# Attention feeding two feed-forward layers on one core: transfers of one tile ordered together, a 64-query product that waits to be seen, running sums stored later, last output tiles in other buffers

## The chip, the cores and the metric

One Trainium2 chip, one of its NeuronCores. The time of a run is device microseconds of that core for one execution of the whole program; the median of several runs is given. The trace is that of one profiled execution.

A core has engines that run their own instruction streams side by side: TensorE (PE in the profile; its weight loads are PEld), VectorE (DVE), ScalarE (ACT), GpSimd (POOL) and SyncE (SP). SP computes nothing here; it issues transfers between HBM and on-chip memory, one after the other, on its own queue (SPq). A few transfers are issued by ACT (ACTq). Each stream is in order: an instruction that waits holds all that stand behind it on its engine. Matmuls write to eight PSUM banks.

## The reference

```python
# q, k, v: (4, 8, 576, 64); s: (4, 8, 576)
cum    = np.cumsum(np.maximum(s, 0.0), axis=-1)
bias   = -(cum[:, :, :, None] - cum[:, :, None, :])
scores = np.where(causal, -1e9, scale * q @ k.T + np.minimum(bias, 0.0))
attn   = softmax(scores);  x = attn @ v          # laid out as (2304 tokens, 512)
x = (x @ w_a * (x @ w_b)) @ w_out                # d_ff 1536
h = x @ w_in                                     # d_ff 2048
out = (np.maximum(h, 0) + alpha * np.minimum(h, 0)) @ w_out2
```

## The kernel before

**Blocks and steps.** The 2304 tokens go through the feed-forward layers in four blocks (512, 512, 512 and 768 tokens). Of every batch of 576 queries, the first 512 belong to a block of their own; the last 64 of all four batches belong to the last block. The first batch's attention runs alone at the start. After it, the attention of later batches is cut into some dozens of steps a block that are put between the feed-forward matmuls of the block before: scores (`s01`, `s23` for 512 queries, `s4` for the last 64, L744), the product with the values (`av`, L804; `av_b` for the 64 queries, L862), all per batch and pair of heads. Every feed-forward matmul is done as three (high by high, low by high, high by low: L1223 to L1225, L1854 to L1856, L1706 to L1708). The last block uses seven products of half-size blocks in place of eight for part of its work.

**The path of a 64-query tile.** `s4` gives scores in PSUM; DVE and ACT make probabilities `z`; DVE turns them in 32x32 blocks into `zt`; SP stores `zt` to a scratch `zd` in HBM and loads it back in another layout as `pb`; `av_b` multiplies `pb` with the values in `vb`. The tile `vb` for a 64-query product is filled by six transfers: four of 32x4x128 (64 KB), two of 32x128 (16 KB). Also loaded on SP: `kq` (queries and keys of a pair of heads), `cb` (running sums, broadcast; `cb0` and `cb1` for the 512 and for the 64 queries), `pt` (as `pb`, for the 512 queries), and `raw` (weights).

**What sets the order.** Nothing schedules at run time. While the program is written out, the class `Order` keeps a clock for each engine from a table of costs and plays the steps through. Work off PE is written as generators (chains): each `yield` names an engine and a cost, and the planner emits the instruction when that engine is next free in its plan. `dma` (L315) takes 480 ns of SP and counts as landed after a planned latency; a chain that fills a tile by several `yield from dma(...)` lines emits the next transfer only after the one before has landed in the plan, and transfers of other chains are emitted between them. `due` (L1259) emits the attention steps that are due among the feed-forward matmuls; it puts a step off by up to four steps while `possible` (L1234) says that the plan has not seen its inputs yet. Before the change `possible` answers yes for `av_b` alone at once: `av_b` is emitted when it is due, and the planned clock is moved on to the time at which its inputs are there. In the program that runs, order is all that is left of the plan: each engine runs its list, with waits on semaphores.

**Eight lanes.** A transfer's landing is signalled on one of eight semaphores (`DMAHW0` to `DMAHW7` in the order's waits) in turn; a transfer on SP waits, before it is issued, until the one before it on its lane has landed.

**Start and end.** `first_attention` stores the running sums `cum` to `cum_d` in HBM (L387) right after DVE has made them, between the loads of `kq`. At the end six output tiles are copied from PSUM to tiles `o` of one tag (`t`, four slots) by ACT and stored by SP; the fifth and the sixth wait until the stores of the first two have landed.

Of the kernel before, what the change touches and what calls it, by code (L numbers as in the profile page):

```python
# [21 lines left out]
P = 128  # L22
D = 64
# [188 lines left out]
def attention_two_moe_kernel(  # L212
# [102 lines left out]
    def dma(o, i):  # L315
        yield {"sp": 480}, 700
        nc.sync.dma_start(o, i)
        yield {"dma": prod(o.shape) / (180 if o.dtype == U16 else 90)}, run.landing

    def split(src, hi, lo, sbuf=True):  # L320
        yield from copy(hi, src, 0.52 if sbuf else 1.04)
        yield from sub(lo, src, f32(hi), sbuf)
# [61 lines left out]
    def running_sums(s_sb):  # L384
        nc.vector.tensor_scalar(s_sb, s_sb, 0.0, 8.0, op0=ALU.max, op1=ALU.mult)
        nc.vector.tensor_tensor_scan(cum[:, 0:S], s_sb, s_sb, 0.0, op0=ALU.add, op1=ALU.max)
        nc.sync.dma_start(cum_d, cum[:, 0:S])  # L387
        nc.vector.tensor_copy(cum[:, S:S + QB], cum[:, QA:S])
        for i in range(0, P, D):
            nc.scalar.activation(cums[i:i + NE], cum[0:NE, 0:QA], AF.Copy)  # L390
            if i == 0:
                nc.vector.tensor_tensor(
                    cums[BH:BH + NE], cum[0:NE, 0:QA], f32(cums[0:NE]), op=ALU.subtract
                )
            else:
                nc.vector.tensor_copy(cums[i + BH:i + BH + NE], f32(cums[BH:BH + NE]))
        bases = acc[3][:, 0:4 * NE].rearrange("p (r b) -> p r b", b=NE)
        for r in range(4):
            nc.tensor.matmul(
                bases[:, r, :], cum[:, r * P:r * P + 1].to_broadcast([BH, P]), ident[:BH, 0:NE],  # L400
                start=True, stop=True,
            )
        nc.vector.scalar_tensor_tensor(
            rows, bases, less[:, 0:1], one_of, op0=ALU.mult, op1=ALU.add
        )
        sums = acc[2][:, 0:NR * BH].rearrange("p (r b) -> p r b", b=BH)
        for r in range(NR):
            nc.tensor.transpose(sums[:, r, :], cum[:, r * P:(r + 1) * P], ident[:BH, :BH])
        nc.vector.tensor_scalar(cumq[:, 0:4, :], sums[:, 0:4, :], -1.0, None, op0=ALU.mult)
        for j in range(2):  # L410
            own = slice(j * QB, (j + 1) * QB)
            nc.vector.tensor_scalar(
                cumq[own, 4, 0:BH // 2], sums[own, 4, j:BH:2], -1.0, None, op0=ALU.mult
            )
# [2 lines left out]
    sizes = [512] * (NT // 512 - 1) + [512 + NT % 512]  # L417
    NB = len(sizes)

    def leave(b, t, o):  # L420
        if t < QA // P:
            yield from dma(out[b * S + t * P:b * S + (t + 1) * P, :], o)
        else:
            ends = [(2 * t - 2 * QA // P + j + 1) * S for j in range(2)]
            halves = [
                run.spawn(dma(out[e - QB:e, :], o[j * QB:(j + 1) * QB]), run.t)
                for j, e in enumerate(ends)
            ]
            for half in halves:
                yield half  # L430
        run.give(of_t, run.t)


    pb_t, scores = {}, []
# [16 lines left out]
    def load_v(b, hp, u):  # L451
        c0 = 2 * hp * D
        got = []

        def chain():
            yield of_vb
            vr = raw.tile([P, 5, 2 * D], F32, name="vb", tag="vb", bufs=VB)
            got.append(vr)
            if b + u >= TURN:
                keys = v[b, 0:QA, c0:c0 + 2 * D].rearrange("(c j k) d -> j k c d", j=4, k=32)  # L460
                if u:
                    yield {"pool": 240}, SEEN
                    nc.gpsimd.memset(vr[:, 4, :], 0.0)
                for j in range(4):
                    yield from dma(vr[j::4, 0:4, :], keys[j])
                    if u and j < 2:
                        k0 = QA + 32 * j
                        yield from dma(vr[j::4, 4, :], v[b, k0:k0 + 32, c0:c0 + 2 * D])
                return
            yield from dma(  # L470
                vr[:, 0:4, :], v[b, 0:QA, c0:c0 + 2 * D].rearrange("(c p) d -> p c d", p=P)
            )
            if u:
                yield {"pool": 240}, SEEN
                nc.gpsimd.memset(vr[QB:P, 4, :], 0.0)
                yield from dma(vr[0:QB, 4, :], v[b, QA:S, c0:c0 + 2 * D])

        v_t[b, hp, u] = got, run.spawn(chain(), slack=SL_QK)

# [19 lines left out]
    def load_kq(b, hp, u):  # L499

        got = []

        def chain():
            if not u and b >= STACK:
                halves = [run.spawn(stack(b, 2 * hp + j, got), run.t) for j in range(2)]
                yield halves[0]
                yield halves[1]
                return
            yield of_kq
            kq = raw.tile([P, 2 * QA], F32, name="kq", tag="kq", bufs=KQ)  # L510
            got.append(kq)
            if u:
                yield from dma(kq[:, 0:S + P], kq_b[b, hp])
            else:
                for j in range(2):
                    own = slice(j * D, (j + 1) * D)
                    yield from dma(kq[own], kq_a[b, 2 * hp + j, own])

        kq_t[b, hp, u] = got, run.spawn(chain())

    def load_sums(b, h, u):

        got = []

        def chain():
            yield of_c1 if u else of_c0
            nk = S if u else QA
            cb = raw.tile([P, nk], F32, name=f"cb{u}", tag=f"cb{u}", bufs=2 if u else CB)
            got.append(cb)
            n = P // (u + 1)  # L530
            for j in range(u + 1):
                bh = b * H + (u + 1) * h + j
                yield from dma(
                    cb[j * n:(j + 1) * n], cum_d[bh:bh + 1, 0:nk].to_broadcast([n, nk])
                )

        cb_t[b, h, u] = got, run.spawn(chain())

# [278 lines left out]
        parts = (x[b % 2][:, hp, :] for x in (xh, xl))  # L817
        x_done[b].append(read_by(at, split(pv, *parts, False)))

    def t4(b, hp, j):  # L820

        if j == 0:
            z_t[b, hp, 4] = probabilities(b, hp, 4)
        z = z_t[b, hp, 4]
        k, n = (QB, P) if j else (P, QA)
        at = slot()
        tp = banks[at][0:k, 0:n]
        for c in range(n // P):
            k0 = j * QA + c * P
            nc.tensor.transpose(tp[:, c * P:(c + 1) * P], z[:, k0:k0 + k], ident)  # L830
        run.pe(n / P * 107)
        if j:
            z_t.pop((b, hp, 4))
            run.give(of_z[4])

        def chain():
            if j == 0:
                yield of_pb
                pb_t[hp] = raw.tile([P, 5 * P], F32, name="pb", tag="pb")
                yield {"pool": 240}, SEEN  # L840
                nc.gpsimd.memset(pb_t[hp][QB:P, QA:5 * P], 0.0)
            o = j * QA
            yield from copy(pb_t[hp][0:k, o:o + n], tp, 1.04)

        e_t[b, hp, 4 + j] = read_by(at, chain())

    def av_b(b, hp):

        turned = b + 1 >= TURN
        if turned:  # L850
            settle((b, hp, 4))
        else:
            run.need(*(e_t.pop((b, hp, 4 + j)) for j in range(2)))
        got, ready = v_t.pop((b, hp, 1))
        run.need(ready)
        pb = pb_t.pop(hp)
        at = slot()
        pv = banks[at][:, 0:QB]
        for c in range(5 if turned else 0):
            for j in range(2):  # L860
                p = pb.rearrange("p (i t n) -> p i t n", i=4, n=32)
                nc.tensor.matmul(  # L862
                    pv[64 * j:64 * j + 64], got[0][:, c, j * D:(j + 1) * D],
                    p[:, 2 * j:2 * j + 2, c, :], start=c == 0, stop=c == 4,
                )
        for c in range(0 if turned else 5):
            for j in range(2):
                o = c * P + j * QB
                nc.tensor.matmul(
                    pv[64 * j:64 * j + 64], got[0][:, c, j * D:(j + 1) * D], pb[:, o:o + QB],  # L870
                    start=c == 0, stop=c == 4,
                )
        run.pe(5 * 107)
        run.give(of_vb)
# [11 lines left out]
    def first_attention():  # L886
# [12 lines left out]
        for i in range(HP + 2):  # L899
# [14 lines left out]
                s23(0, i, 3)  # L914
            if i == FROM_WEIGHTS:
                nc.sync.dma_start(alpha_sb, alpha)
                ahead = AHEAD
                prefetch()
            if i == FROM_LEAD:
# [312 lines left out]
        return all(c.done and c.time <= run.now + 100 for c in chains)  # L1232

    def possible(f, args):  # L1234
        rings = 1 if f == two_av else 2
        if f not in (s01, s23, s4, two_av):
            return True
        if not seen(*(reader[i] for i in ring[:rings] if i in reader)):
            return False
        if f == two_av:  # L1240
# [3 lines left out]
                v_t[a, hp, 0][1], v_t[b, hp, 1][1]  # L1244
            )
        b, hp = args[:2]
        if f == s4:
            return seen(kq_t[b, hp, 1][1], z_t[b, hp, 4][1])
        r = args[2] if f == s23 else 0
# [169 lines left out]
    def ffn_seven(blk, sums):  # L1419
# [226 lines left out]
            return end  # L1646

        def store(t):
            yield of_t
            o = ft.tile([P, DM], F32, name="o", tag="t")  # L1650
            yield from copy(o, (acc + banks[0:2])[t], 1.04, SHRUNK ** 2)
            run.spawn(leave(blk, t, o), run.t)

        def x2_part(o, j, d, c):
            yield from split_by(o, xh[1 - j][:, d, c], xl[1 - j][:, d, c], SHRUNK ** 2)
# [98 lines left out]
    def ffn(blk):  # L1754
# [57 lines left out]
        def store(t):  # L1812
            yield of_t
            o = ft.tile([P, DM], F32, name="o", tag="t")
            yield from copy(o, acc[t], 1.04, SHRUNK ** 2)
            run.spawn(leave(blk, t, o), run.t)

        for f in range(NF1 + 1):
            if f < NF1:
# [140 lines left out]
```

## Time and profile before

| | before |
|---|---|
| median of 3 runs | 991.97 us (991.25 to 992.36) |
| profiled execution | 991.26 us, its span 989.5 us |
| PE busy | 964.1 us, 97% of the span |
| DVE / ACT / POOL busy | 745.3 / 559.3 / 231.9 us |
| mean granted TensorE clock | 0.992 of full speed |
| chain that ended last | PE 94%, DVE 2%, DMA 2%, ACT 2% |

The span runs from the first to the last instruction; the run is 1.8 us longer. Read the share of the chain first, then the list of what PE waited for, then the stretches around these waits. The granted clock is given as a share of full speed: 1.00 is 2.4 GHz, 0.50 is 1.2 GHz. A row of the timeline is: start, busy time, engine, line, operation, output<-input and count, and in brackets the idle time before it and what ended it.

### The profile page before, as it was taken

Reading aid. Unit: us, or ns where it says so; the run is one execution under the profiler, and the core shown is the slowest. Engines: PE = TensorE matmul, PEld = TensorE weight load, DVE = VectorE, ACT = ScalarE, POOL = GpSimd, SP = SyncE. Lnnn points to the kernel's source line nnn. Section 1 sums busy time; section 2 is a strip of 40 time slices with the busy share of each in tenths; the row PEclk is TensorE's granted clock in tenths of the full one; section 3 lists DMA queues with packets and bytes.
Section 4 is the critical chain, followed back from the end, with each engine's and each line's share of the span. In section 5 each row is a group of like instructions: output and inputs, shape, how many; then the busy total and the mean of one; then the engine's idle time right before and its main releaser. Section 6 shows DMA issues by size and latency. Waiting matters only on the chain.

```text
span 989.5 us, 15862 instructions
## 1 busy us (share of the span) xinstructions
PE 964.1 (97%) x5235; PEld 811.8 (82%) x5235; DVE 745.3 (75%) x1725; ACT 559.3 (57%) x1162; POOL 231.9 (23%) x291
## 2 busy tenths in 40 slices
PE   6999999999999999969999999999999999999997
PEld 5577777788888888858888888888899999999896
DVE  7897878868788878847578868666497888788772
ACT  6976767657665657526455547544552333566443
POOL 2130113321155556303235434522100000000000
PEclk9999999999999999979999999999999999999999
DMA  7589997789599978977498786855403223021202
GB/s 191 179 283 320 344 364 248 280 291 320 202 285 297 319 247 280 283 222 231 151 273 252 214 273 195 252 177 176 161 24 105 65 64 103 27 65 65 64 0 65
DMA packets 140115, 196.78 MB, mean 199 GB/s; under 512 B 35776, under 2 KB 79808, under 8 KB 140032
## 3 DMA queue, kind: packets, MB, share of 16 engines
q1 hardware_dynamic: 130240, 177.93, 57.5%
q10 hardware_dynamic: 9792, 17.83, 4.9%
q8 instruction: 41, 0.67, 0.3%
q14 instruction: 42, 0.34, 0.1%
HBM read 152.13 MB, written 43.59 MB: 198 GB/s over the span
## 4 chain that ended last, share of the span: by engine, by line
PE 94%; DVE 2%; DMA 2%; ACT 2%; issue 0%; SPq 0%; ACTq 0%
PE bank L1223 21%; PE bank L1224 21%; PE bank L1225 21%; PE bank L1854 5%; PE bank L1856 4%; PE bank L1855 4%; PE bank L804 3%; PE bank L1707 2%; PE bank L1706 2%; PE bank L1708 2%; PE bank L547 2%; PE bank L744 1%; PE bank L566 1%; PE bank L862 1%; DMA kq<-in_kq_a_dram 1%; ACT z L276 1%
## 5 line engine op out<-in xcount | busy, mean ns | idle before, releaser
L1223 PE MATMUL bank<-xh,wh 128*128 128x512 f32 (+1 forms) x620 | 237.8, 384 | 0.0
L1224 PE MATMUL bank<-xl,wh 128*128 128x512 f32 (+1 forms) x620 | 234.3, 378 | 0.9 <-DVE xl L292 0.9
L1225 PE MATMUL bank<-xh,wl 128*128 128x512 f32 (+1 forms) x620 | 234.1, 378 | 0.0
L284 ACT ACTIVATE wh<-raw 128x512 fp32r<-128x512 f32 (+1 forms) x198 | 115.0, 592 | 91.8 <-PE bank L1224 39.0
L1223 PEld LDWEIGHTS bank<-xh,wh 128*128 128x128 f32 x620 | 116.5, 188 | 25.7 <-issue 6.5
L1224 PEld LDWEIGHTS bank<-xl,wh 128*128 128x128 f32 x620 | 116.6, 188 | 19.9 <-DVE xl L292 1.4
L1225 PEld LDWEIGHTS bank<-xh,wl 128*128 128x128 f32 x620 | 116.5, 188 | 19.4
L301 POOL TENSOR_TENSOR wl<-raw,wh 128x512 fp32r<-128x512 f32 x68 | 92.1, 1359 | 114.7 <-ACT wh L284 82.8
L301 DVE TENSOR_TENSOR wl<-raw,wh 128x512 fp32r<-128x512 f32 (+1 forms) x136 | 84.4, 633 | 39.9 <-ACT wh L284 33.6
L276 ACT ACTIVATE z<-z,mn 128x512 f32<-128x512 f32 (+4 forms) x144 | 83.0, 578 | 36.9 <-DVE mn L292 36.2
L1223 PE MATMUL bank<-gh,wh 128*128 128x512 f32 (+1 forms) x240 | 89.6, 373 | 0.0
L1224 PE MATMUL bank<-gl,wh 128*128 128x512 f32 (+1 forms) x240 | 88.6, 369 | 0.0
L1225 PE MATMUL bank<-gh,wl 128*128 128x512 f32 (+1 forms) x240 | 88.4, 368 | 0.0
L1854 PE MATMUL bank<-wh,gh 128*128 128x512 f32 x192 | 77.8, 405 | 0.0
L284 ACT ACTIVATE gh<-g 128x512 fp32r<-128x512 f32 x84 | 52.8, 628 | 43.1 <-DVE g L292 42.8
L1856 PE MATMUL bank<-wh,gl 128*128 128x512 f32 x192 | 75.5, 393 | 0.0
L1855 PE MATMUL bank<-wl,gh 128*128 128x512 f32 x192 | 75.5, 393 | 0.0
L1004 ACT ACTIVATE top<-raw 128x512 f16<-128x512 bf16 x90 | 69.2, 785 | 7.1 <-DMA raw<-in_w_dram 3.8
L301 DVE TENSOR_TENSOR gl<-g,gh 128x512 fp32r<-128x512 f32 x68 | 51.6, 759 | 18.4 <-ACT gh L284 17.5
L301 POOL TENSOR_TENSOR wl<-w,wh 128x512 fp32r<-128x512 f32 x24 | 31.8, 1323 | 134.8 <-ACT wh L284 92.0
L311 DVE TENSOR_SCALAR z<-z,sm 128x512 f32<-128x512 f32 (+4 forms) x103 | 59.0, 597 | 1.3
L292 DVE STREAM_TRANSPOSE zt<-z 128x384 f32<-128x384 f32 (+2 forms) x88 | 56.2, 650 | 4.8 <-DMA zd<-zt 3.8
(149 smaller groups left out, 1915.0 us busy)
## 6 DMA issues: line engine op xcount, KB each, us to landing
raw<-w_d SPq DMA_DIRECT2D x91, 512.0 KB, 4.3
raw<-in_w_dram SPq DMA_DIRECT2D x90, 512.0 KB, 5.9
w_d<-w ACTq DMA_DIRECT2D x46, 256.0 KB, 5.7
zd<-zt SPq DMA_DIRECT2D x48, 192.0 KB, 4.7
pt<-zd SPq DMA_DIRECT2D x48, 192.0 KB, 5.6
kq<-in_kq_a_dram SPq DMA_DIRECT2D x16, 512.0 KB, 6.1
vb<-in_v_dram SPq DMA_DIRECT2D x112, 64.0 KB, 4.4
zd<-zt SPq DMA_DIRECT2D x24, 256.0 KB, 2.9
```

The source lines that it names most:

```text
L276: nc.scalar.activation(o, i, func, **k)
L284: nc.scalar.activation(o, i, AF.Copy, scale=by)
L292: f(*args, **k)
L301: (nc.gpsimd if eng == "pool" else nc.vector).tensor_tensor(o, i0, i1, op=ALU.subtract)
L311: (nc.gpsimd if eng == "pool" else nc.vector).tensor_scalar(o, i, s0, s1, op0=ALU.mult, op1=ALU.mult)
L1004: nc.scalar.activation(top.bitcast(F16).rearrange("p (n t) -> p n t", t=2)[:, :, 1], r.bitcast(BF16)[:, 4:4 + 4 * WN].rearrange("p (n t) - ...
L1223: nc.tensor.matmul(o, wh, ih, start=first, stop=False)
L1224: nc.tensor.matmul(o, wh, il, start=False, stop=False)
L1225: nc.tensor.matmul(o, wl, ih, start=False, stop=last)
L1854: nc.tensor.matmul(acc[t], gh[:, c], wh, start=first, stop=False)
L1855: nc.tensor.matmul(acc[t], gh[:, c], wl, start=False, stop=False)
L1856: nc.tensor.matmul(acc[t], gl[:, c], wh, start=False, stop=last)
```

## The change

Four edits. First, a helper `dmas` spawns the transfers of one tile together, so that they are emitted one right after the other; it is used for `vb`, for the halves of `kq` and for the two broadcasts of `cb1`. Second, `possible` checks `av_b` too: it is put off until the plan has seen `pb` and `vb` land (by up to four steps). Third, the store of `cum` to `cum_d` moves to the third round of `first_attention`, behind the load of `alpha`. Fourth, the first two of the last six output tiles go to slots of another tag (`d`, free by then) and the last tile is copied and stored in two halves: ACT copies and stores one, DVE copies the other and SP stores it. Code that was never reached (`t4`, the other branch of `av_b`) is dropped.

```diff
+    def dmas(*pairs):
+        sent = [run.spawn(dma(o, i), run.t) for o, i in pairs]
+        for c in sent:
+            yield c
...
     def running_sums(s_sb):
-        nc.sync.dma_start(cum_d, cum[:, 0:S])
...
-                for j in range(4):
-                    yield from dma(vr[j::4, 0:4, :], keys[j])
-                    if u and j < 2:
-                        k0 = QA + 32 * j
-                        yield from dma(vr[j::4, 4, :], v[b, k0:k0 + 32, c0:c0 + 2 * D])
+            pairs = [(vr[j::4, 0:4, :], keys[j]) for j in range(4)]
             if u:
                 yield {"pool": 240}, SEEN
+                nc.gpsimd.memset(vr[:, 4, :], 0.0)
+                for j in range(2):
+                    k0 = QA + 32 * j
+                    pairs.append((vr[j::4, 4, :], v[b, k0:k0 + 32, c0:c0 + 2 * D]))
+            yield from dmas(*pairs)
...
-                for j in range(2):
-                    own = slice(j * D, (j + 1) * D)
-                    yield from dma(kq[own], kq_a[b, 2 * hp + j, own])
+                own = [slice(j * D, (j + 1) * D) for j in range(2)]
+                yield from dmas(*((kq[o], kq_a[b, 2 * hp + j, o]) for j, o in enumerate(own)))
...
                 nc.sync.dma_start(alpha_sb, alpha)
+                nc.sync.dma_start(cum_d, cum[:, 0:S])
...
-        rings = 1 if f == two_av else 2
-        if f not in (s01, s23, s4, two_av):
+        rings = 1 if f in (two_av, av_b) else 2
+        if f not in (s01, s23, s4, two_av, av_b):
             return True
...
+        if f == av_b:
+            return (b, hp, 4) in e_t and seen(e_t[b, hp, 4], v_t[b, hp, 1][1])
...
         def store(t):
-            yield of_t
-            o = ft.tile([P, DM], F32, name="o", tag="t")
-            yield from copy(o, (acc + banks[0:2])[t], 1.04, SHRUNK ** 2)
-            run.spawn(leave(blk, t, o), run.t)
+            slots = of_t if t < QA // P else of_d
+            yield slots
+            if t < QA // P:
+                o = ft.tile([P, DM], F32, name="o", tag="t")
+            else:
+                o = pools["big"]([P, T], F32, "d", 5)[:, 0:DM]
+            src = (acc + banks[0:2])[t]
+            if t + 1 == QA // P:
+                for c in (slice(0, DM // 2), slice(DM // 2, DM)):
+                    run.spawn(last_half(t, o, src, c), run.t)
+                return
...
+        def last_half(t, o, src, c):
+            by_act = c.start == 0
+            if by_act:
+                yield from act(o[:, c], src[:, c], AF.Copy, scale=SHRUNK ** 2)
+            else:
+                yield from dve(
+                    DM // 2, 1.04, nc.vector.tensor_scalar, o[:, c], src[:, c], SHRUNK ** 2, None,
+                    op0=ALU.mult,
+                )
+            rows = out[blk * S + t * P:blk * S + (t + 1) * P, c]
+            yield {"act" if by_act else "sp": 480}, 700
+            (nc.scalar if by_act else nc.sync).dma_start(rows, o[:, c])
```

The first place is on SP, in the second block, where the 64-query tiles of batch 0 begin. The numbers behind the names tell tiles apart; `zd_4905` and `pb_4952` belong to the first pair of heads, `zd_5008` to the second, and `vb_4631` holds the first pair's values. Before:

```order
L317 DMA zd_4905<-zt_4904 128x640
L317 DMA vb_4912<-in_v_dram 32x4x128
L317 DMA vb_4631<-in_v_dram 32x128
L317 DMA vb_4700<-in_v_dram 32x128
L317 DMA raw_4945<-w_d_147 128x2x512
L317 DMA raw_4916<-in_w64_dram 128x2048
L317 DMA cb1_4911<-cum_d_118 64x576
L317 DMA pb_4952<-zd_4905 128x4x160
...
L317 DMA zd_5008<-zt_5007 128x640
L317 DMA vb_4631<-in_v_dram 32x4x128
L317 DMA vb_4700<-in_v_dram 32x4x128
```

The same place now; `zd_4828` and `pb_4886` are the first pair's, whose values `vb_4605` were all sent some twenty transfers earlier, and `vb_4899` is a later pair's:

```order
L317 DMA zd_4828<-zt_4827 128x640
L317 DMA kq_4897<-in_kq_b_dram 128x704
L317 DMA cb1_4898<-cum_d_118 64x576 x2
L317 DMA vb_4899<-in_v_dram 32x4x128 x4
L317 DMA vb_4899<-in_v_dram 32x128 x2
L317 DMA pb_4886<-zd_4828 128x4x160
```

The last transfer of the values that the first product reads stood behind the next tile's `zd_5008`; now all six stand far ahead of it, and between `zd` and `pb` of one tile there are nine transfers in place of six.

The second place is SP two pairs later, between `zd` and `pb` of the third pair. Before:

```order
L317 DMA zd_5133<-zt_5132 128x640
L317 DMA vb_5060<-in_v_dram 32x4x128
L317 DMA raw_5180<-w_d_147 128x2x512
L317 DMA kq_5194<-in_kq_a_dram 128x1024
L317 DMA kq_5195<-in_kq_a_dram 128x1024
L317 DMA cb0_5196<-cum_d_118 128x512
L317 DMA cb0_5197<-cum_d_118 128x512
L317 DMA cb1_5199<-cum_d_118 64x576
L317 DMA pb_5174<-zd_5133 128x4x160
```

And now:

```order
L317 DMA zd_5146<-zt_5145 128x640
L317 DMA raw_5183<-w_d_147 128x2x512
L317 DMA kq_5199<-in_kq_a_dram 128x1024
L317 DMA kq_5200<-in_kq_a_dram 128x1024
L317 DMA cb0_5201<-cum_d_118 128x512
L317 DMA cb0_5202<-cum_d_118 128x512
L317 DMA vb_5203<-in_v_dram 32x4x128 x4
L317 DMA cb1_5204<-cum_d_118 64x576 x2
L317 DMA vb_5205<-in_v_dram 32x4x128 x4
L317 DMA vb_5205<-in_v_dram 32x128 x2
L317 DMA pb_5188<-zd_5146 128x4x160
```

Seven transfers stood between the two; now there are seventeen, because two whole `vb` tiles go ahead of `pb_5188`. For the second pair (`pb_5029`) it was three and is ten.

The third place is PE at the first of these products. Before:

```order
L1854 MATMUL bank4_103<-wh_4775,gh_4827 128x512
L1855 MATMUL bank4_103<-wl_4776,gh_4827 128x512
L1856 MATMUL bank4_103<-wh_4775,gl_4828 128x512
L744 MATMUL bank0_99<-kq_4698 128x288
L744 MATMUL bank1_100<-kq_4698 128x288
L862 MATMUL bank0_99<-pb_4952,vb_4631 64x64 x10
```

And now:

```order
L1185 MATMUL bank3_102<-xh1_108,wh_4767 128x512
L1186 MATMUL bank3_102<-xl1_110,wh_4767 128x512
L1187 MATMUL bank3_102<-xh1_108,wl_4768 128x512
L1185 MATMUL bank3_102<-xh1_108,wh_4767 128x512
L1186 MATMUL bank3_102<-xl1_110,wh_4767 128x512
L1187 MATMUL bank3_102<-xh1_108,wl_4768 128x512
L830 MATMUL bank0_99<-pb_4886,vb_4605 64x64 x10
```

The scores of the second pair (L744) stood right ahead of the first pair's product; they are now 24 feed-forward matmuls ahead of it. The product itself stands 1404 feed-forward matmuls into the program in place of 1407, the scores of the first two pairs at 1335 and 1380 in place of 1359 and 1407, the second, third and fourth product at 1458, 1524 and 1587 in place of 1458, 1521 and 1575.

The fourth place is the start of SP. Before:

```order
L890 DMA s_sb<-in_s_dram 32x576
L317 DMA kq<-in_kq_a_dram 64x1024 x2
L387 DMA cum_d<-cum 32x576
L317 DMA kq<-in_kq_a_dram 64x1024 x3
L317 DMA vb<-in_v_dram 128x4x128
```

And now:

```order
L851 DMA s_sb<-in_s_dram 32x576
L317 DMA kq<-in_kq_a_dram 64x1024 x6
L317 DMA vb<-in_v_dram 128x4x128
L317 DMA kq<-in_kq_a_dram 64x1024 x2
L317 DMA vb<-in_v_dram 128x4x128 x2
```

The store of the sums no longer stands between the loads of `kq`.

## Rows read from the trace of the kernel before

**Rows 1.** The page's part 1, busy time of each engine.

```profile
PE 964.1 (97%) x5235; PEld 811.8 (82%) x5235; DVE 745.3 (75%) x1725; ACT 559.3 (57%) x1162; POOL 231.9 (23%) x291
```

**Rows 2.** What PE waited for: line, releaser, total us, times, longest.

```profile
PE bank L862 <- DMA vb<-in_v_dram: 7.9, 1, 7.9
...
PE bank L771 <- POOL z L311: 1.9, 1, 1.9
```

**Rows 3.** Timeline of PE, the 64-query products of the first three pairs.

```profile
434.66 1.33 PE L862 MATMUL bank<-pb,vb 128*64 128x64 f32 x20 [7.87 <-DMA vb<-in_v_dram]
...
450.89 0.80 PE L862 MATMUL bank<-pb,vb 128*64 128x64 f32 x20
...
467.14 0.80 PE L862 MATMUL bank<-pb,vb 128*64 128x64 f32 x20
```

**Rows 4.** The chain of waits around that stall: start, us, what.

```profile
430.67 0.85 DVE zt L292
...
432.55 2.13 DMA vb<-in_v_dram
434.68 1.32 PE bank L862 x20
...
436.72 0.43 PE bank L1855
...
440.84 0.23 PE bank L1225
```

**Rows 5.** Busy time by stretch: bounds, length, engines, granted clock, DMA share, GB/s.

```profile
21.00:24.00 3.00, 3.00 (x16) 3.00 (x16) 2.97 (x18) 2.38 (x6) 0.69 (x1) 0.50 1.02 407
...
430.00:432.00 2.00, 0.00 (x0) 0.00 (x0) 1.96 (x4) 0.00 (x0) 0.15 (x1) 0.57 0.18 71
```

**Rows 6.** Timeline of SP, around the stall and two pairs later.

```profile
419.83 0.33 SPq L317 DMA_DIRECT2D zd<-zt  x1
...
424.79 2.47 SPq L317 DMA_DIRECT2D vb<-in_v_dram  x4
...
450.21 0.33 SPq L317 DMA_DIRECT2D zd<-zt  x1
...
451.89 0.93 SPq L317 DMA_DIRECT2D kq<-in_kq_a_dram  x2
452.87 1.71 SPq L317 DMA_DIRECT2D cb<-cum_d  x3
456.27 0.37 SPq L317 DMA_DIRECT2D pb<-zd  x1
457.68 5.66 SPq L317 DMA_DIRECT2D vb<-in_v_dram  x3
```

**Rows 7.** DMA issues of the whole run: count, KB each, median us to landing.

```profile
kq<-in_kq_a_dram SPq DMA_DIRECT2D x16, 512.0 KB, 6.1
...
pb<-zd SPq DMA_DIRECT2D x16, 320.0 KB, 4.5
cb<-cum_d SPq DMA_DIRECT2D x32, 144.0 KB, 6.1
...
cb<-cum_d SPq DMA_DIRECT2D x16, 256.0 KB, 6.8
```

**Rows 8.** Landings of the tile pb over the run, shortest, median and longest.

```profile
DMA to landing us min/median/max: 3.0/4.5/8.2
```

**Rows 9.** Timeline of PE, the two waits for kq.

```profile
9.12 0.58 PE L566 MATMUL bank<-kq 64*128 64x128 f32 x1 [0.40 <-DMA kq<-in_kq_a_dram]
...
48.97 0.37 PE L566 MATMUL bank<-kq 64*128 64x128 f32 x1 [0.75 <-DMA kq<-in_kq_a_dram]
```

**Rows 10.** Timeline of all engines at the end.

```profile
982.77 0.39 PE L1708 MATMUL bank<-wh,gl 128*128 128x512 f32 x1
983.45 0.60 ACT L284 ACTIVATE o<-bank 128x512 f32<-128x512 f32 x1 [1.03 <-DMA out_dram<-o]
984.78 0.60 ACT L284 ACTIVATE o<-bank 128x512 f32<-128x512 f32 x1 [0.74 <-DMA out_dram<-o]
```

More of the change, by code (lines that the diff above doesn't have):

```diff
@@ L418, in attention_two_moe_kernel, with leave @@
     NB = len(sizes)
-    def leave(b, t, o):
+    def leave(b, t, o, slots):
         if t < QA // P:
@@ L424, in leave @@
             ends = [(2 * t - 2 * QA // P + j + 1) * S for j in range(2)]
[L425 to L431, printed above, removed]
+            yield from dmas(
+                *((out[e - QB:e, :], o[j * QB:(j + 1) * QB]) for j, e in enumerate(ends))
+            )
+        run.give(slots, run.t)
     pb_t, scores = {}, []
@@ L458, in chain @@
             got.append(vr)
[L459 to L463, printed above, removed]
-                for j in range(4):
-                    yield from dma(vr[j::4, 0:4, :], keys[j])
-                    if u and j < 2:
-                        k0 = QA + 32 * j
-                        yield from dma(vr[j::4, 4, :], v[b, k0:k0 + 32, c0:c0 + 2 * D])
+            if b + u < TURN:
+                yield from dma(
+                    vr[:, 0:4, :], v[b, 0:QA, c0:c0 + 2 * D].rearrange("(c p) d -> p c d", p=P)
+                )
                 return
-            yield from dma(
-                vr[:, 0:4, :], v[b, 0:QA, c0:c0 + 2 * D].rearrange("(c p) d -> p c d", p=P)
-            )
+            keys = v[b, 0:QA, c0:c0 + 2 * D].rearrange("(c j k) d -> j k c d", j=4, k=32)
+            pairs = [(vr[j::4, 0:4, :], keys[j]) for j in range(4)]
             if u:
                 yield {"pool": 240}, SEEN
-                nc.gpsimd.memset(vr[QB:P, 4, :], 0.0)
-                yield from dma(vr[0:QB, 4, :], v[b, QA:S, c0:c0 + 2 * D])
+                nc.gpsimd.memset(vr[:, 4, :], 0.0)
[3 more added lines that the diff above has]
+            yield from dmas(*pairs)
         v_t[b, hp, u] = got, run.spawn(chain(), slack=SL_QK)
@@ L530, in chain @@
             n = P // (u + 1)
[L531 to L534, printed above, removed]
-                )
+            yield from dmas(*(
+                (
+                    cb[j * n:(j + 1) * n],
+                    cum_d[bh:bh + 1, 0:nk].to_broadcast([n, nk]),
+                )
+                for j, bh in enumerate(range(b * H + (u + 1) * h, b * H + (u + 1) * (h + 1)))
+            ))
         cb_t[b, h, u] = got, run.spawn(chain())
@@ L818, in av @@
         x_done[b].append(read_by(at, split(pv, *parts, False)))
[L820 to L845, printed above, removed]
-    def av_b(b, hp):
[L849 to L853, printed above, removed]
+    def av_b(b, hp):
+        settle((b, hp, 4))
         got, ready = v_t.pop((b, hp, 1))
@@ L858, in av_b @@
         pv = banks[at][:, 0:QB]
-        for c in range(5 if turned else 0):
+        for c in range(5):
             for j in range(2):
@@ L864, in av_b @@
                     p[:, 2 * j:2 * j + 2, c, :], start=c == 0, stop=c == 4,
[L865 to L871, printed above, removed]
                 )
@@ L1648, in store @@
         def store(t):
-            yield of_t
-            o = ft.tile([P, DM], F32, name="o", tag="t")
-            yield from copy(o, (acc + banks[0:2])[t], 1.04, SHRUNK ** 2)
-            run.spawn(leave(blk, t, o), run.t)
+            slots = of_t if t < QA // P else of_d
[9 more added lines that the diff above has]
+                return
+            yield from copy(o, src, 1.04, SHRUNK ** 2)
+            run.spawn(leave(blk, t, o, slots), run.t)
+        def last_half(t, o, src, c):
[6 more added lines that the diff above has]
+                    op0=ALU.mult,
+                )
+            rows = out[blk * S + t * P:blk * S + (t + 1) * P, c]
+            yield {"act" if by_act else "sp": 480}, 700
+            (nc.scalar if by_act else nc.sync).dma_start(rows, o[:, c])
         def x2_part(o, j, d, c):
@@ L1815, in store @@
             yield from copy(o, acc[t], 1.04, SHRUNK ** 2)
-            run.spawn(leave(blk, t, o), run.t)
+            run.spawn(leave(blk, t, o, of_t), run.t)
         for f in range(NF1 + 1):
```

## The prediction, made before the changed kernel ran

> **What bounds the kernel now.** I read the page's part 1 first: PE is busy for 97% of the span [rows 1], so the time is PE's own work plus the few places where it waits or runs slowly. The list of what PE waited for comes next. It is short: one wait of 7.9 us of a 64-query product (L862) for a transfer of `vb`, and otherwise waits of at most 2 us outside the first ten microseconds [rows 2]. The third view is the chain around the big wait. There the product starts at 434.66 after 7.87 us of idling [rows 3]; the chain goes back through the landing of `vb` (2.13 us) to the block transpose `zt` on DVE, which ran from 430.67 to 431.52 [rows 4]. The transfer has no use for `zt`. What ties the two together is SP's order: the store `zd` of the next tile, which needs `zt`, stands ahead of the last `vb` transfer, so SP sat from 427.26 (424.79 and 2.47) [rows 6] to 431.5 with `vb` behind it. The reader should see that neither DMA bandwidth nor DVE's load is the trouble, since in 430 to 432 the DMA share is 0.18 [rows 5].
>
> The wait costs more than its length. The granted clock, full before, fell within 430 to 432 (mean 0.57) [rows 5], and the matmuls behind the product are 0.43 us apart where full speed gives 0.23 [rows 4]. From 434.68 to 440.84 are 6.16 us for the product and eleven matmuls; at full speed they take 0.66 (half of 1.32) and 11 x 0.23 = 2.53, together 3.19 [rows 4]. So 2.97 us are lost behind the wait, and 7.87 + 2.97 = 10.84 us in all.
>
> **Together in the order, and the product that waits to be seen.** By the new order all six transfers of the first product's `vb` stand some twenty transfers ahead, so that wait ends: -10.8 us. The number of transfers, their bytes and PE's matmuls are unchanged; I cost the emission itself at nothing, since SP is an issuer with idle stretches, as the one above.
>
> What is late next is `pb`. It comes from `zd` through HBM, stands on SP behind the transfers that were put together, and the product follows as soon as the plan has `pb` landed. I bound the three products of batch 0 from their own rows, in us after `zd`. Prices: a `vb` transfer keeps SP for 2.47/4 = 0.62, a `kq` for 0.93/2 = 0.46, a `cb` for 1.71/3 = 0.57, `zd` 0.33 [rows 6], a weight load about as much as a `cb`; `pb` lands after 4.5 (3.0 to 8.2) [rows 8], `cb1` after 6.1, `kq` after 6.1, `cb0` after 6.8 [rows 7]. A transfer waits, too, for the one about eight earlier: the `vb` at 457.68 came 5.8 after the `kq` at 451.89 and a microsecond after SP was done with `pb` [rows 6]; so lanes count.
>
> First pair: its scores stand 24 matmuls earlier, so `zd` goes at 419.83 - 24 x 0.23 = 414.3 [rows 4, 6]; the product's place is 426.79 (434.66 - 7.87), three matmuls less: 426.1 [rows 3]. That leaves 11.8. The issues need 0.33 + 0.46 + 2 x 0.57 + 6 x 0.62 = 5.6, but `pb` also waits for the second `cb1`, issued at 1.4 and landed at 7.5; with 4.5 it is there at 12.0. Stall 0.2, between 0 and 3.9 (with 8.2).
>
> Second pair: its scores stand 27 matmuls earlier, `zd` at 431.5 - 6.2 = 425.3 if DVE keeps up (it may be 2 to 3 later), the product at 450.89 - 10.84 = 440.05 [rows 3]. That leaves 14.7, or 12. By the same count with a weight load ahead `pb` is there at 13.1. Stall 0.5, between 0 and 4.8.
>
> Third pair: `zd` at 450.21 - 10.84 = 439.4, the product at 467.14 - 10.84 + 0.7 = 457.0 [rows 3, 6]. That leaves 17.6. Here seventeen transfers stand between. The second `kq` goes at 1.4 and lands at 7.5; only then `cb1`, eight behind, goes, and lands at 13.6; only then `pb`, eight behind it. It lands at 18.2 with 4.5, at 21.9 with the 8.2 that the `pb` of just this stretch may be (it shares the queue with the same `kq` and `cb`). Between 0 and 4.3; I take 2.4, with 6.5 for the landing, nearer to a loaded queue. The fourth pair has seven transfers fewer ahead of its `pb` and I give it nothing, nor the later eight products, whose `pb` the new order sends close behind its `zd`.
>
> Sum of the three: +3.1, of which a little is shared since a late second product gives the third more time: I take +3.0, and 0 and 9 as its ends. Waits of 1 to 3 us I charge without a slow clock. That is a choice: after a wait of 1.9 us [rows 2] and a second short one near 20 us the clock was at 0.50 from 21 to 24 [rows 5], so a slow stretch is possible and priced below.
>
> The Trainium skill, page "DMA: Bandwidth & Descriptors", section "Anatomy of one DMA", says that the DMA engines never wait on semaphores, and that any such wait is done by the issuing sequencer before it dispatches. The trace agrees at the idle second half of SP's 427 to 432. By that rule a transfer with its data ready still stands behind each waiting one, and a full queue in front of `pb` counts at its whole length; the sum by it would be the upper ends above, some 986.
>
> **Running sums stored later, kq halves together.** PE's two waits for `kq`, 0.40 at 9.12 and 0.75 at 48.97 [rows 9], come from halves issued apart, the first behind the store of the sums. Both halves now go back to back and no store stands between: -1.2 (bounds 0, if the added traffic lands later, and 2, if the first products also follow on earlier). The store is read by later `cb` loads only; it lies beside PE's work. If it were late, `cb` would be late and DVE's score work with it.
>
> **Last output tiles.** After PE's last matmul (982.77 + 0.39 = 983.16) ACT copies two tiles, at 983.45 after 1.03 us and at 984.78 after 0.74 us, both waiting for stores out of their slots [rows 10]. The new buffers take these waits away: the copy of the fifth tile begins near 982.4 and is over by 983.0, the last one's ACT half can begin at 983.2 and takes about 0.4 (an estimate from 0.60 for the whole), and its DVE half follows it by the new order's semaphore, to about 984.0. Before, the copy ended at 985.38. That is -1.4 and some less for stores of half the size: -1.5 (1.0 to 1.9).
>
> **Sum**, on the profiled execution of 991.26 us (its span of 989.5 and 1.8 around it): -10.8 - 1.2 - 1.5 + 3.0 = -10.5, so 980.8. The median of the runs is 0.7 above that execution, so 981.5.
>
> **Rivals.** (a) `pb` is in time everywhere: the waits that I charge are zero, 991.26 - 13.5 + 0.7 = 978.5. For it: the product is put off until the plan has `pb` landed, and the landing's shortest is 3.0. Against it: the margins above are within a microsecond of the need, and landings spread up to 8.2 [rows 8].
>
> (b) The long wait: at the third pair `pb` lands late by the upper end, 4.3, or the second also, up to 9 together, and the clock falls for some microseconds as it did in rows 4 (up to 3). 978.5 + 5 + 3 = 986.5, up to 990. For it: seventeen transfers in a stretch in which three `vb` took 5.66 us of SP [rows 6]. Against it: the scores of this pair are early.
>
> (c) The change does not do what it says: the plan's landing is not the chip's, and the first product waits for `pb` about as long as it did for `vb`. Only start and end are gained, 991.26 - 2.7 + 0.7 = 989.3. Against it: the landing would have to be some 8 us beyond the longest that the trace has.
>
> (d) Slower: SP's queue, filled by whole tiles, becomes what PE waits for. Each of the first and the third product would wait as before's did and lose its clock, 2 x 10.84 = 21.7, against 13.5 gained: 991.26 + 8.2 + 0.7 = 1000. It decides from 13.5 us of new waits on. Against it: it needs two `pb` 8 us late, where the counts above end at 3.9 and 4.3.
>
> **How the numbers follow.** My forecast (new waits of 1 to 5 us, 979.5 to 984) has 0.50; (a) 0.26, (b) 0.14, (c) 0.05, (d) 0.03, and 0.02 for anything near no change. The range of 977.3 to 987.5 takes in the full gain with the upper bounds of its small terms, and the greater part of (b). A change of 0.2%, 2 us, is about what runs of this kernel can tell from none. Faster by more than that is 0.50 + 0.26 + 0.14 and most of (c), 0.94; within it 0.03; slower 0.03.
>
> **What would show it.** Right: in the list of PE's waits, `vb` at the 64-query product is gone and `pb` stands there with one to three waits, the longest at the third pair; the wait for `kq` is gone or under 0.4; ACT has no wait for a store at the end. SP's timeline shows the six `vb` in one run and `pb` behind them. Wrong: a `vb` wait that stays, a `pb` wait over 4 us with a granted clock near 0.5 behind it, weights late at a feed-forward matmul (L1185 and its neighbours, waiting for `wh` or `wl`), or an end that is as long as before. If the time is under 978, the waits that I charged for `pb` were not there.

## The result and the profile after

The changed kernel takes 1001.96 us (median of 4 runs, 1000.54 to 1003.67) against 991.93 before: ratio 1.0102, 95% interval 1.0088 to 1.0117. It is 10 us slower, where the prediction had it 10 us faster. The profiled execution took 1000.54 us, its span is 998.4 (989.5 before).

What PE waited for, all waits of 0.6 us and more (line, releaser, total us, times, longest), answers to [rows 2]. L830 is the 64-query product, L803 that of the 512 queries, L546 their scores, L1185 and L1186 the feed-forward matmuls; L404 and L770 are transposes in the first batch's attention, whose waits the kernel before had too:

```profile
PE bank L404 <- DVE cum L392: 5.4, 1, 5.4
PE bank L830 <- DMA pb<-zd: 4.6, 1, 4.6
PE bank L546 <- DVE mn L292: 2.8, 2, 1.7
PE bank L803 <- DMA pt<-zd: 2.7, 2, 2.2
PE bank L770 <- POOL z L311: 2.1, 1, 2.1
PE bank L1185 <- DVE g L292: 2.0, 2, 1.5
PE bank L546 <- DVE xl L301: 1.3, 2, 1.1
PE bank L770 <- DVE z L311: 1.1, 1, 1.1
PE bank L1186 <- DVE xl L292: 0.9, 1, 0.9
PE bank L770 <- DVE xl L301: 0.7, 1, 0.7
PE bank L1186 <- POOL gl L301: 0.6, 1, 0.6
```

The wait for `vb` is gone, and so are both waits for `kq`. In their place stand one for `pb`, two for `pt`, and seven for DVE (`mn`, `g`, `xl` of the scores) or POOL that the kernel before did not have. Two places show the mechanism. The first is the third 64-query product, in SP's timeline and in PE's; they answer to [rows 6] and [rows 3]:

```profile
453.98 0.33 SPq L317 DMA_DIRECT2D zd<-zt  x1
454.41 0.38 SPq L317 DMA_DIRECT2D raw<-w_d  x1
454.84 1.12 SPq L317 DMA_DIRECT2D kq<-in_kq_a_dram  x2
456.01 0.91 SPq L317 DMA_DIRECT2D cb<-cum_d  x2
457.07 9.12 SPq L317 DMA_DIRECT2D vb<-in_v_dram  x4
466.24 1.24 SPq L317 DMA_DIRECT2D cb<-cum_d  x2
467.52 3.93 SPq L317 DMA_DIRECT2D vb<-in_v_dram  x6
471.49 0.58 SPq L317 DMA_DIRECT2D pb<-zd  x1
```

```profile
474.96 1.34 PE L830 MATMUL bank<-pb,vb 128*64 128x64 f32 x20 [4.63 <-DMA pb<-zd]
476.23 0.80 PE L1840 MATMUL bank<-wh,gh 128*128 128x512 f32 x1
476.82 0.63 PE L1841 MATMUL bank<-wl,gh 128*128 128x512 f32 x1
```

From `zd` to `pb` SP needs 17.5 us. Four `vb` transfers, whose issue takes 2.5, take 9.1: SP waits between them. What it waited for from 456 to 467 us (total, times, longest):

```profile
SPq L317 <- DMA w_d<-raw: 4.4, 1, 4.4
SPq L317 <- DMA raw<-w_d: 1.9, 1, 1.9
```

No `vb` transfer reads `raw` or `w_d`; these are the transfers before it on its lane. The store `w_d` is issued by ACT, whose transfers take their turn on the same eight lanes. The product waits 4.63 us and PE runs slowly after it.

The second is the chain of waits that ended at 362 us (start, us, what):

```profile
343.27 7.47 DMA cb<-cum_d
...
350.80 6.46 DMA zd<-zt
...
357.36 0.06 DVE zt L292
...
361.76 0.70 DVE xl L301
...
362.51 0.74 PE bank L546 x2
```

A store `zd` leaves SP at 350.80 only when an earlier `cb` has landed, lands 6.46 us later, and until then the buffer of `zt` is not free. DVE's next transpose waits for it, and DVE's in-order line holds the subtraction `xl` that the scores need.

The longest waits of this stretch, 1.71 and 1.07 us for `mn` at 377 and 378 us, have no `zd` in the chain that leads to them from 362.51 on. In it DVE and ACT had waited for a weight tile:

```profile
366.10 0.79 ACT L966 ACTIVATE top<-raw 128x512 f16<-128x512 bf16 x1 [3.33 <-DMA raw<-in_w_dram]
...
366.92 0.69 DVE L292 SCALAR_TENSOR_TENSOR raw<-raw,top 128x512 int32<-128x512 int32 x1 [2.75 <-ACT top L966]
```

The clock, by stretch (bounds, length, engines, granted clock, DMA share, GB/s), answers to [rows 5]. It falls three times in this kernel's middle, at each place where PE waited longest:

```profile
370.00:380.00 10.00, 7.22 (x32) 5.77 (x31) 8.64 (x19) 5.80 (x13) 5.53 (x6) 0.93 0.82 273
...
420.00:430.00 10.00, 7.32 (x70) 5.57 (x69) 4.90 (x8) 3.75 (x7) 3.43 (x6) 0.83 1.00 344
...
470.00:480.00 10.00, 5.37 (x31) 4.18 (x30) 4.31 (x8) 1.93 (x5) 1.97 (x3) 0.71 0.79 269
```

The end, ACT and PE, answers to [rows 10]: no wait for a store is left.

```profile
991.02 1.97 ACT L284 ACTIVATE o<-bank 128x512 f32<-128x512 f32 x3
993.08 0.38 ACT L276 ACTIVATE o<-bank 128x256 f32<-128x256 f32 x1
...
992.65 0.39 PE L1694 MATMUL bank<-wh,gl 128*128 128x512 f32 x1
```

**The ledger.** The feed-forward matmuls come in the same order and number in both kernels, so the start of the n-th tells how late the changed kernel is. At the first it is 1.55 us early. It loses 1.84 by 67 us (a `g` behind a transpose that waited for `zd`), 0.78 near 165, 7.0 between 355 and 399 (1.4 at the scores of 362, 4.6 at the waits for `mn` and the slow clock behind them, 1.0 near 399, again behind a `zd`), 7.4 at the third product. Between these, around 424 to 445, it gains 5.7 net: the old stall's 10.8, less 5.2, by difference, of a new wait for `pt` (2.23 and 0.45) and its slow clock. From the last matmul's end to the span's end are 5.4 us (998.4 - 993.04) for 6.3 before. In all -1.55 + 1.84 + 0.78 + 7.04 - 5.66 + 7.43 - 0.98 = +8.9, the difference of the spans.

### The profile page after: what moved, and what is told of

It reads as the page before. It is cut to its first block, busy times and chain, and to the rows that moved or that the text cites. A ratio compares the mean times of both kernels' runs of the same rounds, so it can differ in the third digit from the quotient of the medians.

```text
span 998.4 us, 15852 instructions
## 1 busy us (share of the span) xinstructions
PE 968.7 (97%) x5235; PEld 812.2 (81%) x5235; DVE 741.6 (74%) x1708; ACT 560.2 (56%) x1173; POOL 235.5 (24%) x298
## 4 chain that ended last, share of the span: by engine, by line
PE 87%; DVE 5%; DMA 5%; ACT 2%; issue 1%; SPq 0%; POOL 0%; ACTq 0%; DVEq 0%; POOLq 0%
PE bank L1185 19%; PE bank L1186 19%; PE bank L1187 19%; PE bank L1840 5%; PE bank L1841 4%; PE bank L1842 4%; DMA zd<-zt 3%; PE bank L1693 2%; PE bank L1692 2%; PE bank L1694 2%; PE bank L803 2%; PE bank L546 2%; PE bank L743 1%; DVE z L292 1%; PE bank L565 1%; PE bank L830 1%
## 5 line engine op out<-in xcount | busy, mean ns | idle before, releaser
L1185 PE MATMUL bank<-xh,wh 128*128 128x512 f32 (+1 forms) x620 | 238.3, 384 | 2.0 <-DVE g L292 2.0
L1186 PE MATMUL bank<-xl,wh 128*128 128x512 f32 (+1 forms) x620 | 234.7, 379 | 0.9 <-DVE xl L292 0.9
L1185 PEld LDWEIGHTS bank<-xh,wh 128*128 128x128 f32 x620 | 116.8, 188 | 28.3 <-issue 6.5
L1186 PEld LDWEIGHTS bank<-xl,wh 128*128 128x128 f32 x620 | 116.7, 188 | 19.9 <-DVE xl L292 1.3
L301 POOL TENSOR_TENSOR wl<-raw,wh 128x512 fp32r<-128x512 f32 x74 | 98.8, 1338 | 101.8 <-ACT wh L284 88.5
L1185 PE MATMUL bank<-gh,wh 128*128 128x512 f32 (+1 forms) x240 | 89.6, 374 | 0.0
L1186 PE MATMUL bank<-gl,wh 128*128 128x512 f32 (+1 forms) x240 | 88.7, 369 | 0.6 <-POOL gl L301 0.6
L292 DVE SCALAR_TENSOR_TENSOR w<-raw,top 128x512 int32<-128x512 int32 x68 | 46.9, 703 | 19.7 <-ACT top L966 17.2
```

Of the source, the lines that this page charges most:

```text
L292: f(*args, **k)
L301: (nc.gpsimd if eng == "pool" else nc.vector).tensor_tensor(o, i0, i1, op=ALU.subtract)
L1185: nc.tensor.matmul(o, wh, ih, start=first, stop=False)
L1186: nc.tensor.matmul(o, wh, il, start=False, stop=False)
```

## The experiments

Each ran with its own runs of the kernel before (medians 992.0 to 992.7). Two theories. Q: the transfers that are now sent early stand in SP's line ahead of `zd`, `pt` and `pb`, and what is late there makes PE and, through `zt`'s buffers, DVE late. P: the waits come from the other edits, which move steps on DVE and PE.

One thing needs no run, only the order. With the part of the check that asks for `vb` taken out of the changed kernel, the order on every engine stays as it is: with `vb` sent together the check never puts a product off for `vb`. With the whole check taken out, the first two products of batch 0 stay where they are, the third stands 3 feed-forward matmuls earlier and the fourth 12.

**vb apart** (label e1_vb_apart).

```diff
-            yield from dmas(*pairs)
+            for j in range(4):
+                yield from dma(vr[j::4, 0:4, :], keys[j])
...
```

> The changed kernel with one edit undone: the transfers of a vb tile are sent one by one again, each when the plan has the one before landed; kq and cb halves stay together, the 64-query product still waits until seen, start and end as changed. Theory Q (the run of six vb transfers on SP holds up zd, pt and pb behind it, and through zd DVE): the waits of 1.5 us at 64 us, 7 us at 362 to 399, 5.8 us at 424 and 7.4 us at 475 go, and the 64-query product is put off until its vb is there: 978 to 984 us. Rival P (the waits come from the other edits, which move DVE's and PE's steps): they stay, 990 to 1002 us.

985.53 us, ratio 0.9935 (0.9919 to 0.9951). One edit undone gives back 16 us, so Q holds for the most part; `pt` no longer waits, `pb` 0.9 us at most. A wait for DVE's `mn` remains in the 362 to 399 stretch, so it misses the expected range by a little:

```profile
PE bank L546 <- DVE mn L292: 3.4, 2, 2.8
```

It is no shorter than in the changed kernel (2.8), so this part of the 7.0 us there is not the work of `vb` together.

**Start and end alone** (e3_ends): the changed kernel with vb and cb one by one and without the check.

> The kernel before with only the start and the end changed (running sums stored later, kq halves together, last output tiles in other buffers and in halves). Both theories: the wait of 7.9 us for vb stays with its slow clock, the two waits for kq go, the end is 1.0 us shorter: 991.9 - 1.6 - 1.0 = 989.3 us (988.5 to 990.5). If the 1.8 us that the changed kernel lost at 64 us come from the start and not from vb, 991 us.

987.90 us, 0.9956 (0.9939 to 0.9974), 4.2 us off the medians, somewhat better than the expected range: in its trace the feed-forward begins 2.8 us earlier than before, and the stall is there:

```profile
PE bank L828 <- DMA vb<-in_v_dram: 7.6, 1, 7.6
```

**Start, end and the check** (e4_seen_ends): as the last, with `possible` asking for `av_b`.

```diff
+        if f not in (s01, s23, s4, two_av, av_b):
+        if f == av_b:
+            return (b, hp, 4) in e_t and seen(e_t[b, hp, 4], v_t[b, hp, 1][1])
```

> As the kernel with only start and end changed, and the 64-query product waits until seen; vb and cb transfers one by one as before. Theory Q: the product is put off behind its vb, the stall of 10.8 us shrinks or goes and nothing new is late: 978 to 984 us. Rival P (the check itself shifts steps so that others are late): 986 to 1000 us, with new waits at scores and products of the 512 queries.

978.16 us, 0.9859 (0.9844 to 0.9875): faster than both kernels. All that PE waits for in it (0.6 us and more), the first wait being the program's start:

```profile
PE bank L404 <- DVE cum L392: 5.4, 1, 5.4
PE bank L768 <- POOL z L311: 2.1, 1, 2.1
PE bank L1184 <- DVE xl L292: 0.9, 1, 0.9
PE bank L768 <- DVE z L311: 0.8, 1, 0.8
PE bank L768 <- DVE xl L301: 0.7, 1, 0.7
```

SP's timeline of it, around the first two pairs, shows that the values still come late, and behind the next `zd`:

```profile
423.76 2.44 SPq L317 DMA_DIRECT2D vb<-in_v_dram  x3
429.78 0.34 SPq L317 DMA_DIRECT2D zd<-zt  x1
430.22 0.41 SPq L317 DMA_DIRECT2D raw<-in_w_dram  x1
430.68 1.91 SPq L317 DMA_DIRECT2D vb<-in_v_dram  x3
```

SP still idles from 426.2 to 429.8 with `vb` behind `zd`. The product simply stands 51 feed-forward matmuls later (1458 in place of 1407) and starts at 435.48 without a wait. It was PE's order that had to give, not SP's.

**The check alone** (e11_seen_only): the kernel before with that check and nothing else.

> The kernel before with the second edit alone: the 64-query product waits until the plan has seen pb and vb land; every transfer is sent as before, start and end as before. With start and end also changed the check brought 987.9 down to 978.2 us, 9.7. If the edits add up: 992.3 - 9.7 = 982.5 us (981 to 984), with no wait at the 64-query products and the two waits for kq left. If the check needs the changed start to help: 986 us or more.

983.67 us, 0.9905 (0.9880 to 0.9931), in the range for edits that add up. Its profiled execution has no wait at the 64-query products, and 2.5 us for `kq`, with a stretch of half clock behind it that the kernel before does not have there: its feed-forward begins 3.1 us later than before, and gains 9.9 from there to the last feed-forward matmul.

**vb issued by ACT** (e6_vb_act): the same plan, another issuer.

```diff
-        nc.sync.dma_start(o, i)
+        (by or nc.sync).dma_start(o, i)
```

> The changed kernel with the same order of everything, except that ACT and not SP issues the vb transfers (152 of SP's 620; they take some 0.4 us of ACT each). Theory Q in its narrow form (it is SP's issue time and its waiting in line): zd, pt and pb are issued some 4 us earlier at each run of six, the four groups of waits go, and ACT's extra time stays off PE's path: 978 to 984 us. If it is not SP's line but the bytes in flight or the eight lanes that the transfers share, or the plan's order on DVE, the waits stay: 995 to 1004 us.

1017.37 us, 1.0240 (1.0206 to 1.0274), the worst of all and outside both ranges. (The traces show 144 `vb` transfers that change their issuer, not the 152 of the expectations.) The narrow form of Q is wrong: it is not the issue time alone. The line has moved to ACT, which now waits for earlier transfers to land with its own work behind it. What ACT waited for (two of its rows):

```profile
ACT wh L284 <- DMA vb<-in_v_dram: 23.9, 5, 7.9
...
ACT gh L284 <- DMA vb<-in_v_dram: 10.7, 3, 4.5
```

`pt` now waits 0.2 us and `pb` 1.8, but DVE's `mn` and `xl`, behind ACT, hold the scores for 12.8. ACT's transfers take the same eight lanes as SP's, so this run does not take `vb` out of the lanes.

**vb issued by POOL** (e10_vb_pool): the same edit with `nc.gpsimd`, whose transfers use lanes of their own.

> The changed kernel with the same planned order, but the vb transfers are issued by POOL, through its own queue and its own eight lanes; SP's line and lanes lose 152 of 620 transfers, the bytes stay. Theory Q': zd, pt and pb no longer stand behind vb; the waits at 424 and 475 us (pt, pb) are gone or under 1 us, and DVE's waits for zd shrink; what it costs is POOL's time (its subtractions later): 980 to 992 us. Rival (bytes in flight, or the plan's order on DVE and PE): pt and pb as late as in the changed kernel, 998 us or more.

982.51 us, 0.9898 (0.9880 to 0.9916). The transfers, their bytes and the plan are those of the changed kernel, and 19 of its us are gone. SP's timeline at the third pair, and PE's waits in this kernel after the first 60 us:

```profile
441.29 0.33 SPq L317 DMA_DIRECT2D zd<-zt  x1
441.71 0.38 SPq L317 DMA_DIRECT2D raw<-w_d  x1
442.14 1.00 SPq L317 DMA_DIRECT2D kq<-in_kq_a_dram  x2
443.19 3.23 SPq L317 DMA_DIRECT2D cb<-cum_d  x4
451.48 0.38 SPq L317 DMA_DIRECT2D pb<-zd  x1
```

```profile
PE bank L546 <- DVE mn L292: 1.1, 1, 1.1
PE bank L1186 <- DVE xl L292: 0.9, 1, 0.9
...
PE bank L1185 <- DVE g L292: 0.5, 1, 0.5
```

From `zd` to `pb` are 10.2 us in place of 17.5, and no product waits. So the transfers of `vb` did the harm by where they stood, not by their bytes. The Trainium skill, page "DMA: Bandwidth & Descriptors", section "Issuing engines are not separate DMA queues", says that issuing from several engines saves only the sequencer's time to initiate them, usually small beside the transfer itself. Here the measurement differs: the issuer decided between 1017, 1002 and 983 us. An issuer also does the waiting, as ACT's rows show.

**cb apart** (e7_cb_apart): the changed kernel with cb1 one by one.

> The changed kernel with the two cb1 broadcasts of a pair of heads sent one by one again; vb stays together. The run before showed that cb1 together costs 7.4 us when vb is apart (985.5 against 978.2). Theory Q' (each transfer that is sent early stands on SP with an unlanded lane in front of it and holds up the stores and loads of the probabilities): vb together costs most of the loss by itself, 990 to 999 us. Rival (cb1 is the culprit and vb only adds to it): 978 to 986 us.

1003.94 us, 1.0117 (1.0099 to 1.0135), a miss a little above the expected range: vb together does the harm by itself, 25.8 us with cb1 apart (1003.9 against 978.2). In its trace DVE waits up to 7.6 us for `zd`. cb1 together costs 7.4 us when vb is apart (985.5 against 978.2), and nothing when vb is together (1002.0 against 1003.9). So the losses do not add; that each is a margin lost at some place or other is my reading, not shown.

**vb by POOL, cb apart** (e12_vb_pool_cb_apart).

> The kernel with the vb transfers together but issued by POOL, and the two cb1 broadcasts sent one by one again. With cb1 together it ran 982.5 us, with waits for DVE of 1.6 us in the 362 to 399 us stretch. Theory Q' (what stands in SP's line counts): with cb1 apart these waits go and the start gains 1.1 us more, as it did when vb was apart: 978 to 981 us. If cb1 together does harm only together with vb on SP: 982 to 983 us.

986.31 us, 0.9939 (0.9918 to 0.9959), a miss on both sides: slower than with cb1 together. The products do not wait, but scores and feed-forward matmuls between 300 and 399 us wait 4.9 us for DVE. So the theory explains `pt` and `pb`, and not every wait for DVE there.

**Lanes in the plan** (e9_lanes): on the changed kernel, the plan holds SP until the transfer eight before has landed.

```diff
+        landed.append(max(run.t, run.free.get("dma", 0.0)) + t + run.landing)
+        if len(landed) >= 8:
+            run.free["sp"] = max(run.free["sp"], landed[-8])
```

> The changed kernel with one thing more in the plan: after each transfer on SP the plan lets the next one start only when the transfer eight before it has landed in the plan. The transfers, their grouping and all costs stay. Theory Q' says that the plan places products and transposes too early because it does not see this wait: the plan now puts DVE's and PE's steps later or other transfers first, and part of the 23 us of new waits goes: 985 to 996 us. Rival (it is the chip's landing times, longer than the plan's, that make things late, and the lanes do not matter): 998 to 1004 us.

997.52 us, 1.0060 (1.0039 to 1.0081): some 4 us better than the changed kernel, and between what the two sides expected. `pb` still waits 4.6 us in two waits. A plan that knows these lanes helps a little. It counts SP's transfers alone, though ACT's take lanes too, so a plan that knows all of them is untested.

**vb in pairs** (e8_vb_pairs).

> The changed kernel with the vb transfers sent two by two, each pair when the plan has the pair before landed (cb1 and kq together as changed). Theory Q': a run of two holds the line a third as long as a run of six, and the time lies between vb apart (985.5) and vb together (1002): 986 to 994 us, with the wait for pt or pb at the 64-query products smaller than 4.6 us. Rival (the position of vb in the order, not the length of its run): as the changed kernel, 998 to 1004 us.

989.65 us, but its ten runs spread from 985.51 to 996.16, ratio 0.9983 (0.9960 to 1.0006). What this kernel computes is not the reference's result, for a cause that is open. Its time is no evidence, and I build nothing on it.

## Why the prediction was wrong

**The bound and the stall: right, a little high.** The wait for `vb` and its clock were counted at 10.8 from [rows 3, 4]. The check alone removed the wait and took 8.4 us off the medians (9.9 behind the start), and 9.7 on top of start and end (987.9 to 978.2).

**Start and end: right in kind.** -1.55 against -1.2, and -1.0 against -1.5, in the changed kernel; alone they gave 4.2 where 2.7 were counted. So it is partly luck that check, start and end together gave 13.9 where the three terms summed to 13.5: one term was too high, the others too low.

**Who removes the stall: not separated.** The prediction credited "together in the order, and the product that waits to be seen" jointly. The check suffices; and with vb together it has nothing to do at the first product.

**The step that failed** is the sentence "I cost the emission itself at nothing, since SP is an issuer with idle stretches, as the one above." SP's idle stretch was a wait of the transfer at the head of its line, which holds all behind it, and not spare room. Sent together, vb cost 16 us (985.5 to 1002). Of the changed kernel's new losses 15 us lie outside the three `pb` that were counted, at 67, 165, 355 to 399 and 424 us. For some 9 of them the trace shows `pt` late (424 us) or DVE behind a late `zd` (67, 362 and 399 us); the 4.6 at 377 us came with a late weight tile and remain with vb apart, and the 0.8 near 165 are not explained. The prediction read only the products of batch 0 and gave "nothing" to the rest; it did not ask what a `zd` that is late does to DVE, though DVE's transpose waits for `zd` in the trace of before, too, for 3.8 us.

**The three products: one mechanism right, its size off.** First and second pair: 0.2 and 0.5 charged, none waited. Third pair: 2.4 charged, 4.63 measured, just above the upper end of 4.3, and with the slow clock 7.4. That it came out near the upper end is partly luck: `pb` was counted to leave 13.6 us after `zd` and to take up to 8.2 to land; it left after 17.5 and landed in 3.1. What held it was not the landing of `kq` and `cb1` but SP's line: 4.4 us for ACT's store `w_d`, and from 464.94 on the issue of ten transfers, 6.5 us. "Waits of 1 to 3 us I charge without a slow clock" fell too: at 377 and at 424 us two waits of together 2.8 and 2.7 us lowered it.

**The rivals.** Rival (d), SP's queue filled by whole tiles, gave 1000 us and 0.03. Its mechanism is what happened; of its two places one is right (the third product), and the rest came as many smaller waits, which the point of 13.5 us of new waits did allow. Its argument against, that two `pb` would have to be 8 us late, priced one form of it only.

**Open.** Whether it is SP's line or the shared lanes that costs most was not told apart by a run: POOL's issue takes vb out of both. At the third pair the trace shows both, 6.3 us of waits for lanes and 6.5 of issue behind them. In the run with POOL `pb`, too, waits 5.0 us for a `w_d` before it leaves. The waits between 355 and 399 us depend on the order in a way that e12_vb_pool_cb_apart shows is not understood.

## What to carry to other kernels

Before transfers are pulled together or earlier on an in-order issuing queue, list what then stands behind them there, stores above all, and who waits for the buffers that these stores free. An idle issuer is no proof of room: look at what it is waiting for. Where a consumer waits for a late input in a static order, moving the consumer back past work that is ready (here 51 matmuls) can be worth more than moving the input forward.

## What the runs showed of the hardware

The engine that issues a transfer also waits for an earlier one to land, and its own work waits with it: with the same plan, 144 transfers issued by ACT, SP and POOL gave 1017, 1002 and 983 us. The earlier one need not be its own: SP held a `vb` transfer for 4.4 us until a store that ACT had issued was down. A PE wait of 4.63 us cost 7.4 with the half clock behind it, and two waits of 2.7 us in all cost 5.2 by difference; a wait of 1.51 us at 64 us left the clock at full speed.
